# Maxima three steps ahead of the scores, dense couples in the lead-in, pv in pairs at the end

## The chip, the cores and the metric

The kernel runs on one core of one Trainium2 chip. The metric is device time of one execution in microseconds. The kernel before took 1690.04 us as the median of three runs (1687.92 to 1691.31). Names used below: PE is the matrix engine (PEld its weight loads), DVE the vector engine, ACT the scalar engine, POOL the GpSimd engine, SP the engine that issues nearly every DMA, in program order, on one queue.

## What is computed

One transformer block with adaptive layer norm, 2048 tokens of 512 channels, 32 heads of 16 channels, an MLP of 1792:

```python
mod = (_silu(c) @ w_mod).reshape(c.shape[0], 6, 1, -1)
sa, ca, ga, sb, cb, gb = (mod[:, i] for i in range(6))
h = _layernorm(x) * (1 + ca) + sa
q, k, v = split_heads(h @ wqkv)                  # 32 heads of 16
p = _softmax(einsum("bhqd,bhkd->bhqk", q, k) * 16 ** -0.5)
x = x + ga * (merge_heads(einsum("bhqk,bhkd->bhqd", p, v)) @ wo)
h = _layernorm(x) * (1 + cb) + sb
x = x + gb * (mish(h @ w1 + b1) @ w2)            # mish(y) = y * tanh(softplus(y))
```

## The kernel before

**Items and steps.** An item is 512 queries of four heads; there are 32, n = 0 to 31, and each has 16 steps, so t runs from 0 to 511. A step takes 128 keys: four score matmuls of 64 array rows each (L618), one for each head, into four banks of a ring of six PSUM banks; ACT takes the exponential of each bank (L621, tile pr); two steps later the four value matmuls add p·v into the item's accumulator (pv, L636, tiles of 32 columns over all 128 rows).

**Maxima.** The softmax's row maximum is subtracted inside the score matmul: two extra rows of the query tile qa hold its negative as a high and a low part. So an item's maxima must be ready before its first score. They come from a second set of products (max_tile, L569), four to a step, which also go to ring banks and which DVE reduces (L571). Step t makes those of step tm = t + PRO, with PRO = 16 + LEAD, LEAD = 4: maxima run 20 steps ahead. When the last four of an item are reduced, neg_max and max_rows make the rows: a transpose on PE (L598, the only matmul out of ident and mm), ACT writes the high part mh (L600), DVE the low part mt, and four DMAs of SP (L607) put them into qa.

**Dense work beside.** The projections, the output projection and most of the MLP are cut into units of twelve 512-column products. In the main loop a unit is done over two steps as 64-row halves (mm_half, L134; all upper halves in one step, lower ones in the next), a half beside a score or a maximum, as 64-row matmuls in the two halves of the array run together; six slots of a step hold such halves, where there is a unit. Where there is none a step has f = 0: scores stand beside maxima instead, four slots.

**The lead-in.** Steps t = -PRO to -1 have no scores. Each makes two max_pair (L583: two 64-row products into two banks, one DVE reduce L585 over both) and after each step's two pairs whole_units issues CREDIT = 7.2 dense products over all 128 rows (L127). The units there are given by the list plan: slices of v, K and q. When a K or q unit is complete its fin runs: ACT copies the accumulator into qf (L258, one buffer), POOL makes the high part qh and the low part ql (L93, L96, two buffers each), and two hooks later SP writes them out (kscr<-qh and kscr<-ql, L272, L273). Hooks are functions run at a half-step h (two to a step), in order of program; they set the order of the DMAs on SP. Six slices of w1 are split early, in the exponentials' still idle buffers (early_prep, L1488 the load, L1496 the stores).

**What sets the order.** Instructions are written in each engine's order by step(); nothing reorders them. A ring bank is taken in turn, and free_banks, run at the end, removes false dependencies between ring users whose banks differ, looking back over the last 32 of them.

## Time and profile before

| quantity | value |
|---|---|
| median of three runs | 1690.04 us |
| the profiled execution's own time | 1688.32 us |
| its span in the trace | 1686.5 us |
| granted PE clock, mean | 0.999 |
| DMA, mean over the span | 142 GB/s |

The profiled time is the span and 1.8 us around it. Rows of the timeline read: start, duration, engine, line and operation, output <- inputs, array rows*columns for a matmul, shape, count; in brackets the idle time before it and what ended that. A duration of a matmul includes its pipeline, so the cost of one in a stream is read from the distance between starts.

### The profile page before, as it was taken

The page shows a single profiled execution, that of the slowest core. Times are in us where ns is not written, and L with a number is a line of the kernel's source. Part 1 is how long each engine was busy: PE and PEld are TensorE (multiplying, and loading weights), DVE is VectorE, ACT ScalarE, POOL GpSimd, SP SyncE. Part 2 cuts the span into 40 slices and gives each one's busy share as a digit, 9 for nine tenths or more (in the row PEclk, how much of TensorE's full clock was granted, in tenths as well). Part 3 has the DMA queues.
Part 4 walks back from the last instruction along what each step waited for, and adds up shares of the span by engine and source line. Part 5 has one row for each costly group of instructions (what it writes and reads, how often), then busy time and mean ns, then how long its engine had stood idle before and what let it go on. Part 6 is the DMA issues. An engine that isn't in the chain of part 4 may idle for free.

```text
span 1686.5 us, 33920 instructions
## 1 busy us (share of the span) xinstructions
PE 1670.4 (99%) x12491; PEld 924.4 (55%) x12491; DVE 1432.9 (85%) x2372; ACT 1357.4 (80%) x2612; POOL 812.5 (48%) x839
## 2 busy tenths in 40 slices
PE   8999999999999999999999999999999999999998
PEld 6755655555445455555555455555555455555687
DVE  6998888888999988888889888888889888883377
ACT  7257777777778988888878998888878988889674
POOL 5555224655313664556323565556323664555442
PEclk9999999999999999999999999999999999999999
DMA  8877656777755334434355434534344433534261
GB/s 261 264 251 188 157 145 197 205 228 218 225 136 161 97 93 104 120 81 130 82 137 161 106 77 98 139 80 122 100 133 120 130 93 81 149 97 135 76 227 63
DMA packets 114983, 239.00 MB, mean 142 GB/s; under 512 B 24500, under 2 KB 50120, under 8 KB 108864
## 3 DMA queue, kind: packets, MB, share of 16 engines
q1 hardware_dynamic: 114808, 236.82, 49.7%
q8 instruction: 99, 1.62, 0.4%
q14 instruction: 68, 0.56, 0.1%
q10 hardware_dynamic: 8, 0.00, 0.0%
HBM read 180.48 MB, written 51.45 MB: 138 GB/s over the span
## 4 chain that ended last, share of the span: by engine, by line
PE 92%; DVE 3%; ACT 2%; DMA 1%; issue 1%; POOL 0%; SPq 0%; ACTq 0%; DVEq 0%; POOLq 0%
PE bk L636 29%; PE ring L618 22%; PE ring L569 19%; PE bk L134 11%; PE bk L127 3%; PE ring L127 2%; PE ring L1249 2%; DVE mx L571 2%; ACT pr L621 1%; PE ring L583 1%; DMA qa<-mt 0%; PE ring L952 0%; PE ring L598 0%; DMA xt<-in_A_x 0%; PE ring L134 0%
## 5 line engine op out<-in xcount | busy, mean ns | idle before, releaser
L571 DVE TENSOR_REDUCE mx<-ring 128x1 f32<-128x512 f32 x1968 | 1221.9, 681 | 150.9 <-PE ring L569 136.2
L621 ACT ACTIVATE pr<-ring 128x512 f32<-128x512 f32 x2048 | 1078.7, 603 | 207.8 <-PE bk L134 116.3
L569 PE MATMUL ring<-ka,qa 64*128 64x512 f32 x1968 | 818.3, 429 | 1.3 <-ACT pr L621 1.0
L618 PE MATMUL ring<-qa,ka 64*128 64x512 f32 x2048 | 759.0, 402 | 3.2 <-ACT pr L621 2.0
L636 PE MATMUL bk<-pr,vg 128*32 128x512 f32 x4096 | 545.1, 604 | 0.0
L569 PEld LDWEIGHTS ring<-ka,qa 64*128 64x128 f32 x1968 | 350.6, 184 | 326.4 <-DVE mx L571 251.4
L618 PEld LDWEIGHTS ring<-qa,ka 64*128 64x128 f32 x2048 | 373.6, 184 | 192.2 <-DVE mx L571 113.3
L134 PE MATMUL bk<-h,w 64*128 64x512 f32 (+1 forms) x1080 | 277.8, 390 | 0.0
L134 PE MATMUL bk<-w,a_h 64*128 64x512 f32 x632 | 210.8, 413 | 0.0
L134 PEld LDWEIGHTS bk<-h,w 64*128 64x128 f32 x1080 | 178.5, 184 | 9.2 <-ACT pr L621 1.5
L636 PEld LDWEIGHTS bk<-pr,vg 128*32 128x32 f32 x4096 | 81.2, 108 | 135.8 <-issue 126.5
L134 PE MATMUL bk<-w,a_l 64*128 64x512 f32 x316 | 124.0, 392 | 0.0
L134 PEld LDWEIGHTS bk<-w,a_h 64*128 64x128 f32 x632 | 106.7, 184 | 3.4 <-ACT hb L830 0.8
L1008 POOL TENSOR_TENSOR y<-yd,y 128x512 f32<-128x512 f32 x44 | 56.8, 1292 | 88.9 <-ACT yd L1007 79.5
L842 POOL TENSOR_SCALAR qq<-ee 128x512 f32<-128x512 f32 x25 | 15.5, 620 | 169.3 <-ACT ee L836 169.3
L858 POOL TENSOR_TENSOR qq<-qq,rr 128x512 f32<-128x512 f32 x42 | 54.1, 1289 | 85.8 <-ACT rr L852 85.8
L844 POOL TENSOR_TENSOR hb<-hb,ee 128x512 f32<-128x512 f32 x42 | 54.1, 1288 | 79.6 <-DVE ee L840 77.6
L134 PE MATMUL bk<-w,o_hl 64*128 64x512 f32 x288 | 79.3, 405 | 0.0
L96 POOL TENSOR_TENSOR a_l<-hb,a_h 128x512 fp32r<-128x512 f32 x53 | 73.1, 1379 | 4.4
L134 PEld LDWEIGHTS bk<-w,a_l 64*128 64x128 f32 x316 | 58.3, 184 | 2.8
L93 POOL TENSOR_SCALAR qh<-qf 128x512 fp32r<-128x512 f32 x27 | 16.7, 620 | 88.3 <-ACT qf L258 68.1
L134 PE MATMUL bk<-h_h,wl 64*128 64x512 f32 x168 | 57.3, 421 | 0.2 <-ACT pr L621 0.2
(222 smaller groups left out, 1901.3 us busy)
## 6 DMA issues: line engine op xcount, KB each, us to landing
ka<-kscr SPq DMA_DIRECT2D x124, 384.0 KB
w<-w2scr SPq DMA_DIRECT2D x56, 512.0 KB
w<-w1scr SPq DMA_DIRECT2D x46, 512.0 KB
vg<-vscr SPq DMA_DIRECT2D x32, 552.0 KB
qa<-qscr SPq DMA_DIRECT2D x124, 100.0 KB
kscr<-qh SPq DMA_DIRECT2D x16, 512.0 KB
qscr<-qh SPq DMA_DIRECT2D x32, 256.0 KB
w2scr<-hl SPq DMA_DIRECT2D x14, 512.0 KB
```

The source lines that it names most:

```text
L96: (nc.gpsimd if eng == "p" else nc.vector).tensor_sub(lo, src, hi.bitcast(F32))
L127: nc.tensor.matmul(acc, l, r, start=start, stop=stop)
L134: i = nc.tensor.matmul(acc, l[64 * g:64 * g + 64], r[64 * g:64 * g + 64], start=start and not then, stop=bool(stop and then))
L569: nc.tensor.matmul(pm, qt[64 * s:64 * s + 64, qs * P:(qs + 1) * P], kt[64 * s:64 * s + 64, kb * TB:(kb + 1) * TB], start=True, stop=True)
L571: nc.vector.tensor_reduce(out=mxs[n][:, s, 4 * j + qs, kb:kb + 1], in_=pm, op=ALU.max, axis=AX.X)
L618: nc.tensor.matmul(p_, kt[64 * s:64 * s + 64, kc * P:(kc + 1) * P], qt[64 * s:64 * s + 64, :], start=True, stop=True)
L621: e = nc.scalar.activation(pr, p_, AF.Exp, scale=SCALE)
L636: nc.tensor.matmul(accs[n][32 * h:32 * h + 32, :], vgs[n][:, o:o + 32], pts.pop((t, h)), start=(kc == 0), stop=(kc == 15))
L844: (nc.vector if tail else nc.gpsimd).tensor_mul(hb, hb, ee)
L858: nc.gpsimd.tensor_mul(qq, qq, rr)
L1008: nc.gpsimd.tensor_add(y[i], yd, y[i])
L1249: nc.tensor.matmul(po[i // 2][:, i % 2, :], l[:, s], w[:, r, :], start=(f == 0 and j == 0), stop=(f == FT - 1 and j == 2))
```

## The change

- **LEAD is 3.** The maxima lead by 19 steps, the lead-in has 19 steps. As 19 is odd, the couple of steps that share a row block of maxima (tm even, tm odd) no longer coincides with the couple of steps (t even, t odd) that shares a dense unit; the number of maxima that stand alone (others) is kept from the first step of a maxima couple to its second. In item 1 one couple of steps takes its maxima column by column, since half of them were made in the lead-in.
- **Dense work of the lead-in.** whole_units is no longer used there. lanes() yields 64-row half slots, each a pair of matmuls of two accumulators in the two halves of the array; dense_slots takes up to four after every max_pair. Twelve 512-column products make one bank of work (take); two such banks are a couple, which goes through twice: turn(c, 0), and turn(c, 1) with the halves exchanged. Between them a small ACT copy (seen) of a pair of maxima banks is what the second pass waits for. Six couples take the same units as before, four accumulators being in use: two ring banks, "ms" and "acc". The ring has four banks until t = -1.
- **Order of units.** The q unit of plan goes ahead of the twelve v units. Two entries of LATE_SPLIT/LATE_LOAD go away.
- **pv in pairs.** In the last PRO steps (t > T - PRO) a step does no pv at an even t; at an odd t, ahead of the third own score, it does those of t-3 and t-2.
- **Three early slices, not six**, two hooks later; the other three join the chain of start_preps. The windows of clear, store_at and load_at move by two hooks.
- **free_banks looks back over 96** ring users instead of 32.

```diff
-    LEAD = 4
+    LEAD = 3
-    CREDIT = 7.2
-    LATE_SPLIT = {3: -8, 4: 4}
-    LATE_LOAD = {3: -15, 4: -4, 5: 9}
+    LATE_SPLIT = {4: 4}
+    LATE_LOAD = {4: -4, 5: 9}
...
-        b = ring_at[0] % NRING
+        b = ring_at[0] % ring_of[0]
...
-                for j, b, others, theirs in seen[-32:]:
+                for j, b, others, theirs in seen[-96:]:
...
         nc.vector.tensor_reduce(out=mxs[n][:, :, jq, kb:kb + 1], in_=pm, op=ALU.max, axis=AX.X)
+        if waiting:
+            seen = ap.tile([P, 2], F32, tag="seen", name="seen", bufs=2)
+            e = nc.scalar.copy(seen, pm[:, :, 0])
+            for c in waiting:
+                c["after"] = e
+            waiting.clear()
...
+    COUPLES = 6
+    now, waiting = [0], []
+    beds = [ring_t[:, NRING - 2, :], ring_t[:, NRING - 1, :], "ms", "acc"]
+
+    def lanes():
...
+        def turn(c, p):
+            (a, fa), (b, fb) = c["two"]
+            for j, both in enumerate(zip(a, b)):
+                for k in range(max(len(x) for x in both)):
+                    for x, g in zip(both, (p, 1 - p)):
+                        if k < len(x):
+                            mm_half(x[k], g, c["after"] if p and not j and not k else None, p)
+                yield len(a) - j - 1
+            if not p:
+                waiting.append(c)
+                return
+            for fin in fa + fb:
+                at(now[0] + 1, lambda fin=fin, h=now[0] + 1: fin(h))
+
+        for _ in range(COUPLES // 2):
+            c1 = yield from couple()
+            yield from turn(c1, 0)
+            c2 = yield from couple()
+            yield from turn(c2, 0)
+            yield from turn(c1, 1)
+            yield from turn(c2, 1)
...
                 max_pair(tm // 16, jq, kb)
-            if second and tm % 16 == 15:
-                neg_max(tm // 16)
-            run_hooks(2 * t + 1)
+                if i and tm % 16 == 15:
+                    neg_max(tm // 16)
+                if not i:
+                    run_hooks(2 * t + 1)
+                dense_slots(2 * t + 1, 4)
             for f in ats.pop(t, []):
                 f()
-            whole_units(2 * t + 1, CREDIT)
...
         if tm < T:
-            o = max(0, (8 - f) // 2)
+            o = mst["others"] = max(0, (8 - f) // 2) if tm % 2 == 0 or not t else mst["others"]
...
-        mid = False
+        mid = t > T - PRO
...
+            if t > T - PRO and second and i < len(mine) and mine[i] is third:
+                pv(t - 3)
+                pv(t - 2)
...
-    plan = [(-PRO, 2, 0, range(4, 16)), (-PRO, 0, 1, (0,)), (-PRO, 1, 1, range(NB)), (-PRO, 1, 2, range(NB)),
+    plan = [(-PRO, 0, 1, (0,)), (-PRO, 2, 0, range(4, 16)), (-PRO, 1, 1, range(NB)), (-PRO, 1, 2, range(NB)),
...
-    EARLY = 6
+    EARLY = 3
```

New lines shift the numbers: in the kernel after, the scores' exponential is L629 (before L621), the qf copy L260 (L258), mh L608 (L600), the rows of maxima L615 (L607), a maximum's product L571 (L569), a score L626 (L618), pv L644 (L636), a dense half L133 (L134), and the kscr writes L274 and L275 (L272, L273).

Three places show how the order moved. The first is ACT where the main loop begins: after the rows of maxima of item 0 (mh) come the copies of finished units into qf, and the exponentials of the first steps (pr). Before:

```order
L600 ACTIVATE mh<-ring 32x128
L258 COPY qf<-bk 128x512 x3
L621 ACTIVATE pr<-ring 128x512 x8
L89 CAST wh<-wr 128x512
L621 ACTIVATE pr<-ring 128x512 x7
```

And after:

```order
L590 COPY seen<-ring 128x2 x2
L608 ACTIVATE mh<-ring 32x128
L260 COPY qf<-ring 128x512 x2
L260 COPY qf<-bk 128x512 x2
L629 ACTIVATE pr<-ring 128x512 x8
```

Four copies stand ahead of the first exponential instead of three; the last two couples are finished together, so all four belong to units that end at the same place, where before a unit ended every few visits.

The second is SP at the same time. mt are the rows of maxima; vg the first item's values; qa and ka the second pair of queries and keys; wm the first two pieces of w_mod; kscr<-qh and kscr<-ql the writes of finished K units. Before:

```order
L607 DMA qa_101<-mt 2x4x128
L230 DMA wr<-in_A_wqkv 128x4x128
L272 DMA kscr<-qh 128x2x512
L273 DMA kscr<-ql 128x512
L556 DMA vg<-vscr 128x1104
L309 DMA qa_103<-qscr 50x512 x2
L318 DMA ka_701<-kscr 48x2048 x2
L730 DMA wm<-in_w_mod 128x4x256 x2
L272 DMA kscr<-qh 128x2x512
L273 DMA kscr<-ql 128x512
L272 DMA kscr<-qh 128x2x512
```

And after:

```order
L615 DMA qa_101<-mt 2x4x128
L558 DMA vg<-vscr 128x1104
L311 DMA qa_103<-qscr 50x512 x2
L320 DMA ka_701<-kscr 48x2048 x2
L738 DMA wm<-in_w_mod 128x4x256 x2
L274 DMA kscr<-qh 128x2x512
L275 DMA kscr<-ql 128x512
```

The K unit whose write stood between the rows of maxima and the vg load is gone from there: all four remaining K writes (three more such pairs follow these rows) come behind the loads of vg, qa, ka and wm.

The third is PE in the main loop, the first step that has dense halves after steps that had none (t = 128 before, t = 126 after). Before:

```order
L569 MATMUL ring<-ka_701,qa_103 128x512 x2
L134 MATMUL bk<-w_5827,o_hl 128x512
L618 MATMUL ring<-qa_101,ka_99 128x512
L134 MATMUL bk<-w_5827,o_hl 128x512
L569 MATMUL ring<-ka_701,qa_103 128x512
L134 MATMUL bk<-w_5827,o_hl 128x512
L618 MATMUL ring<-qa_102,ka_700 128x512
L134 MATMUL bk<-w_5858,o_hl 128x512
L569 MATMUL ring<-ka_701,qa_103 128x512
L134 MATMUL bk<-w_5858,o_hl 128x512 x2
L618 MATMUL ring<-qa_101,ka_99 128x512
L636 MATMUL bk<-pr,vg 32x512 x4
```

And after:

```order
L133 MATMUL bk<-w_5980,o_hl 128x512
L626 MATMUL ring<-qa_104,ka_702 128x512
L133 MATMUL bk<-w_5980,o_hl 128x512
L626 MATMUL ring<-qa_100,ka_98 128x512
L133 MATMUL bk<-w_5980,o_hl 128x512
L133 MATMUL bk<-w_6009,o_hl 128x512
L626 MATMUL ring<-qa_104,ka_702 128x512
L133 MATMUL bk<-w_6009,o_hl 128x512 x2
L626 MATMUL ring<-qa_100,ka_98 128x512
L571 MATMUL ring<-ka_701,qa_103 128x512 x4
L644 MATMUL bk<-pr,vg 32x512 x4
```

Four maxima that stood between scores and halves now stand by themselves behind the step's halves, just ahead of pv.

More of the change, by code (lines that the diff above doesn't have):

```diff
@@ L147, in adaln_block @@
     ring_at = [0]
+    ring_of = [NRING]
     kept = []
@@ L1308, in whole_units, with take, couple, dense_slots @@
                 cur["fin"] = None
+    COUPLES = 6
+    now, waiting = [0], []
+    beds = [ring_t[:, NRING - 2, :], ring_t[:, NRING - 1, :], "ms", "acc"]
+    def lanes():
+        def take():
+            bed = bank(beds[0])
+            beds.append(beds.pop(0))
+            slots, fins = [], []
+            while len(slots) < 12:
+                while not units or now[0] < units[0][0]():
+                    yield None
+                half = len(fins) * TB // 2
+                unit = units.pop(0)[1]
+                fins.append(unit(bed[:, half:]))
+                n = 2 if pe_queue[0][0].shape[-1] <= TB // 2 else 1
+                ms = [(*m[:3], m[3] and half == 0, m[4] and len(slots) * n + len(pe_queue) == 12 * n) for m in pe_queue]
+                slots += [ms[j:j + n] for j in range(0, len(ms), n)]
+                pe_queue.clear()
+            return slots, fins
+        def couple():
+            a = yield from take()
+            b = yield from take()
+            return {"two": (a, b)}
+        def turn(c, p):
[18 more added lines that the diff above has]
+            yield from turn(c2, 1)
+    lane = lanes()
+    def dense_slots(h, most):
+        now[0] = h
+        for _ in range(most):
+            if not next(lane, 0):
+                return
     def maxima(n, u, s, others):
         j, qs = divmod(u, 4)
+        if (n, u) == (1, PRO % 16 // 2):
+            return ([max_tile(n, j, v, qs, kb) for kb in (2, 3)] for v in (s, 1 - s))
         return ([max_tile(n, j, s, qs, kb) for kb in range(4 - others)],
```

25 lines of the change are left out of this document (18 added, 7 removed).

## The prediction

> **What bounds the kernel now.** I read the page first, for the engine that never rests and for the chain that ended last.
>
> ```profile
> span 1686.5 us, 33920 instructions
> ...
> PE 1670.4 (99%) x12491; PEld 924.4 (55%) x12491; DVE 1432.9 (85%) x2372; ACT 1357.4 (80%) x2612; POOL 812.5 (48%) x839
> ...
> PE bk L636 29%; PE ring L618 22%; PE ring L569 19%; PE bk L134 11%; PE bk L127 3%; PE ring L127 2%; PE ring L1249 2%; DVE mx L571 2%; ACT pr L621 1%; PE ring L583 1%; DMA qa<-mt 0%; PE ring L952 0%; PE ring L598 0%; DMA xt<-in_A_x 0%; PE ring L134 0%
> ```
>
> PE is the bound, and the chain is made of PE instructions. So an edit costs what it adds to PE's slots or what it makes PE wait for. Then I took the stretches that the change touches, as windows: the lead-in; the vg issue to the first wm in use; five congested microseconds; the last steps. Columns are microseconds, busy time of PE, PEld, DVE, ACT and POOL, the granted clock, the DMA share and GB/s.
>
> ```profile
> 47.46:98.95 51.49, 51.37 (x298) 36.61 (x298) 47.55 (x44) 9.82 (x22) 29.87 (x28) 1.00 0.84 274
> 96.16:108.72 12.56, 11.94 (x77) 7.06 (x75) 11.57 (x17) 8.14 (x16) 5.09 (x6) 1.00 1.02 280
> 460.00:465.00 5.00, 4.79 (x31) 1.95 (x30) 4.72 (x10) 4.15 (x9) 0.00 (x0) 1.00 1.01 367
> 1532.00:1584.20 52.20, 52.20 (x397) 25.82 (x400) 8.03 (x13) 45.81 (x89) 30.37 (x29) 1.00 0.21 72
> ```
>
> The lead-in takes 51.49 us with PE full and DVE nearly; in the second stretch the DMA engines are full (share 1.02); in the last, PE is full again.
>
> **1. The lead-in gets shorter, by about 5.5 us.** The unit of cost is the distance between starts in PE's timeline, and DVE's reduce.
>
> ```profile
> 89.26 0.28 PE L598 MATMUL ring<-ident,mm 128*32 128x128 f32 x1
> ...
> 98.95 0.50 PE L618 MATMUL ring<-qa,ka 64*128 64x512 f32 x1
> ...
> 111.69 1.06 PE L636 MATMUL bk<-pr,vg 128*32 128x512 f32 x8
> 112.69 0.50 PE L569 MATMUL ring<-ka,qa 64*128 64x512 f32 x1
> ...
> 113.03 0.39 PE L618 MATMUL ring<-qa,ka 64*128 64x512 f32 x1
> ...
> 113.26 0.39 PE L569 MATMUL ring<-ka,qa 64*128 64x512 f32 x1
> ...
> 114.58 1.07 PE L636 MATMUL bk<-pr,vg 128*32 128x512 f32 x8
> ```
>
> ```profile
> L585 DVE TENSOR_REDUCE mx<-ring 128x2 f32<-128x1024 f32 x40 | 46.9, 1219 | 3.1 <-PE ring L583 2.5
> ```
>
> A slot of two 64-row matmuls costs 113.26 - 113.03 = 0.23 us. After, a visit is one max_pair (one slot) and four dense slots: 5 x 0.23 to 0.24 = 1.18 us on PE; DVE needs 46.9 / 40 = 1.17 us for its reduce, so the two run level. Before, a visit takes 51.49 / 40 = 1.29 us: the dense work is the same, but changes of shape between 64 and 128 rows go away. There are 38 visits instead of 40. The dense work, 144 slots, lasts for 36 of them: 36 x 1.18 = 42.5; of the last two, bare pairs that DVE limits (2 x 1.17), PE runs one ahead: 1.2. One new stall stands against it. The weights of the first large K unit (wl) are split on POOL behind the early slices:
>
> ```profile
> 63.54 0.62 POOL L93 TENSOR_SCALAR ep<-ep 128x512 fp32r<-128x512 f32 x1 [8.22 <-DMA ep<-in_B_w]
> ...
> 74.43 1.29 POOL L96 TENSOR_TENSOR wl<-wr,wh 128x512 fp32r<-128x512 f32 x1 [3.01 <-ACT wh L89]
> ```
>
> The q unit comes first and the v units follow, so the K unit is wanted at visit 16, 47.5 + 16 x 1.18 = 66.4. POOL gets the first early slice at 63.5, then has a high part (0.62) and a low part (1.29, as wl's) for it, as much for the q unit, and wl: 63.5 + 1.95 + 1.95 + 1.3 = 68.7, gaps included. Stall 2.2 us. So PE begins step 0 at 47.46 + 42.5 + 1.2 + 2.2 = 93.4 instead of 98.95: -5.5 us. Without the stall it would be -7.7, with DVE setting every visit and none run ahead -4. Item 0's transpose stands behind visit 34: 47.46 + 34 x 1.18 + 2.2 = 89.8 (before 89.26).
>
> **2. Then the main loop waits, which eats that and costs 11 us more.** ACT has four qf copies ahead of the first exponential. qf has one buffer, so the last copy waits for POOL's low part of the unit before it; that low part stands on POOL behind the same unit's high part; qh has two buffers, so that high part waits for a DMA, the kscr write of the unit two back. On SP this write now stands behind vg, qa, ka and wm. PE can issue its first dozen products of step 0, then the ring is full of scores that nothing has read. SP, POOL and ACT at this place before:
>
> ```profile
> 91.77 2.79 SPq L607 DMA_DIRECT2D qa<-mt  x4
> ...
> 95.16 0.45 SPq L272 DMA_DIRECT2D kscr<-qh  x1
> ...
> 96.16 1.01 SPq L556 DMA_DIRECT2D vg<-vscr  x1
> ...
> 99.17 1.62 SPq L730 DMA_DIRECT2D wm<-in_w_mod  x2
> 100.88 0.78 SPq L272 DMA_DIRECT2D kscr<-qh  x1
> ```
>
> ```profile
> 100.04 0.62 POOL L93 TENSOR_SCALAR qh<-qf 128x512 fp32r<-128x512 f32 x1 [1.89 <-DMA kscr<-qh]
> ...
> 108.72 1.89 POOL L734 TENSOR_TENSOR wm<-wm,sil 128x1024 f32<-128x1024 f32 x1 [2.32 <-DMA wm<-in_w_mod]
> ```
>
> ```profile
> 99.13 0.59 ACT L258 COPY qf<-bk 128x512 f32<-128x512 f32 x1 [3.06 <-PE bk L127]
> 99.62 2.07 ACT L621 ACTIVATE pr<-ring 128x512 f32<-128x512 f32 x4
> ```
>
> ```profile
> ka<-kscr SPq DMA_DIRECT2D x124, 384.0 KB
> ...
> vg<-vscr SPq DMA_DIRECT2D x32, 552.0 KB
> qa<-qscr SPq DMA_DIRECT2D x124, 100.0 KB
> kscr<-qh SPq DMA_DIRECT2D x16, 512.0 KB
> ...
> wm<-in_w_mod SPq DMA_DIRECT2D x8, 512.0 KB
> ```
>
> The POOL row at 100.04 shows the dependency at work before: a high part that waits 1.89 us for the kscr write of 95.16, the one that stood ahead of vg. The exponentials did not care, since the last copy (99.13) was already done. After, the transpose at 89.8 lets SP issue the rows of maxima 2.5 us later (as 91.77 against 89.26), 2.8 us long, and vg at 95.2. From the vg issue to the first wm in use was 108.72 - 96.16 = 12.56 us before, with a write of 768 KB (95.16 and its low part) still ahead in the queue, which at the 280 GB/s of that window is 2.8 us: 9.8 us without it. Behind the first wm come the second and the write, 512 KB each: 1.05 MB / 280 = 3.7 us. So the write has landed at 95.2 + 9.8 + 3.7 = 108.7. POOL's high and low part take 1.95, ACT's copy 0.6: first exponential at about 111.2, against 99.62. That is +11.6; since PE has most of step 0 done by then, about 0.6 comes back: **+11.0 us** for the main loop against before, the gain of part 1 included. By the 367 GB/s of the best window the same sum gives 9.6 - 2.1 + 2.9 = 10.4 from the vg issue, first exponential at 108.1, +8. With the queue slower than 280 by a tenth and the transpose 1.5 us later it is +14. I keep +6 to +14, and take 280 as it is this very stretch.
>
> By the Trainium skill ("DMA: Bandwidth & Descriptors", section "Anatomy of one DMA"), whose fit is for DMAs issued by GpSimd, one DMA takes about 2.0 us and its bytes at 436 GB/s. As an estimate by that page the 3.1 MB from vg to the write would land 9.2 us after the vg issue, the first exponential would come at 107.0, and the sum of part 2 would be +7 instead of +11. No window here moved 436 GB/s; the fullest shows 367.
>
> **3. Ten-slot steps: +3.9 us.** Where dense work comes back after steps without it, five times in the loop, the kept number of lone maxima leaves a step with six dense slots and four maxima behind them: 10 slots instead of 7. 5 x 3 x 0.23 = 3.45. At the five opposite changes a step without dense has 7 slots instead of 4:
>
> ```profile
> L571 DVE TENSOR_REDUCE mx<-ring 128x1 f32<-128x512 f32 x1968 | 1221.9, 681 | 150.9 <-PE ring L569 136.2
> ```
>
> ```profile
> 439.29 1.06 PE L636 MATMUL bk<-pr,vg 128*32 128x512 f32 x8
> ...
> 442.01 1.07 PE L636 MATMUL bk<-pr,vg 128*32 128x512 f32 x8
> ```
>
> Such a step takes 2.72 us, nearly a full one's 114.58 - 111.69 = 2.89, though it has four slots fewer; DVE's four reduces (681 ns each in the group's row, 2.72 us) set it. Seven slots, the values (1.0) and some 0.2 for changes of shape (part 4) are 2.81: +0.09 each, +0.45. If waiting DVE and ACT already leave room in a ten-slot step, +1; if the four lone maxima queue at DVE, each 0.68, less 4 x 0.23 of PE, +7.
>
> **4. The end: -1.5.** The lead-in has one step of maxima less, so the loop has one step more that carries them, 2.89 us instead of the 2.59 that these rows show: +0.3. And pv in pairs takes one stretch of values in two away, on some 9 pairs of steps.
>
> ```profile
> 1543.06 1.07 PE L636 MATMUL bk<-pr,vg 128*32 128x512 f32 x8
> ...
> 1545.65 1.06 PE L636 MATMUL bk<-pr,vg 128*32 128x512 f32 x8
> ```
>
> Going over to values and back costs what the starts beside it lie further apart than 0.23: 113.03 - 112.69 = 0.34 behind the values, some 0.1 more than a slot, and I take as much ahead of them: 0.2. 9 x 0.2 = -1.8. PE is busy 52.20 of 52.20 us there, ACT 45.81, so PE's gain counts, unless eight values at once leave the ring full: -2.5 to -0.5.
>
> **5. Item boundaries: +1.** Between the rows of maxima and the item's first score there are now two steps, not three.
>
> ```profile
> 1022.68 0.28 PE L598 MATMUL ring<-ident,mm 128*32 128x128 f32 x1
> ...
> 1031.49 0.49 PE L618 MATMUL ring<-qa,ka 64*128 64x512 f32 x1
> ```
>
> ```profile
> 1023.66 2.76 SPq L607 DMA_DIRECT2D qa<-mt  x4
> ```
>
> From transpose to score it was 8.8 us; now 5.9. The fourth DMA is issued 3.7 us after the transpose, which leaves 2.2 for it to land. That holds on an empty queue. Where the queue is full it was late already:
>
> ```profile
> 369.97 7.91 DMA qa<-mt
> ```
>
> That row of the chain (start, duration) is an item whose rows came after 7.91 us. The step less makes such an item up to 2.9 later; two or three lie in the congested stretch, some of it hidden: +1, from 0 to +5. Three early slices fewer move 2.3 MB of loads and stores out of the lead-in into the chain of preparations, which ends long before its results are needed: 0. The longer look-back can only remove waits; I count 0 here and give it a rival.
>
> Sum against the profiled execution: 11.0 + 3.9 + 0.3 - 1.8 + 1 = +14.4, or 1688.3 + 14.4 = 1702.7. The median of the runs lies 1.7 above the profiled one: 1704. What the measurement can tell from no change is about 0.2%, 3.4 us.
>
> **Rivals.**
> - B, no stall: the exponentials are not held, as the write lands before it is wanted. The main loop then starts 5.5 us early, -5.5 + 3.9 + 0.3 - 1.8 + 1 = -2.1: 1688. Against it stands the order on SP and the full queue; for it only that PE could run late enough, which would need vg's issue 10 us ahead of the last copy.
> - C, faster: the look-back of 96 frees false waits. A step with dense takes 2.89 us; its seven slots, the values (112.69 - 111.69 = 1.0) and 0.2 for the changes of shape make 7 x 0.23 + 1.2 = 2.81. Over some 470 such steps that is -38 at most; with the stall, half of it (-19) decides and gives 1685, and on top of B a tenth gives 1684. Against it: PE stands idle for 16 us of the whole span (1686.5 - 1670.4), and the waits freed must be on users more than 32 back.
> - D, much slower: the rows of maxima come late at every item. From 5.9 us on for the landing, each boundary waits; with 1 us at 20 items +20, 1724; at most 2.9 x 31 = +90. For it: 7.91 us in one item. Against it: 3.7 us of issue leave 2.2 to land on most.
>
> **How the numbers follow.** A (stall of 6 to 14 us, 1697 to 1710) 0.70, since its chain of waits is written in the order and its price is from the same stretch; B 0.10; C 0.08; D 0.12. Range: 1690 to 1714, which leaves out C, half of B and half of D beyond it. Faster by over 0.2%: C and half of B, 0.12; within: half of B and a mild stall, 0.06; slower: the rest, 0.82.
>
> **What would show it.** After, PE's timeline has a gap of over 10 us in step 0, ended by ACT pr, and ACT's qf copy ahead of it is released by POOL ql, and POOL's qh by DMA kscr<-qh. Step 0's first score is near 93.4. Five steps have four maxima alone and take 3.6 us. The chain holds DMA qa<-mt at a few items only. If the gap is missing, B holds; if steps in the middle are shorter than 2.89, C; if each item's first score waits, D.

## The result

The kernel after takes 1739.97 us (median; 1734.42 to 1743.09), the kernel before 1690.0: a ratio of 1.0297, 95% interval 1.0275 to 1.0319. It is 50 us slower, where 14 were forecast and 1714 was the end of the range. The page of the profile after:

```profile
span 1738.2 us, 34382 instructions
...
PE 1682.5 (97%) x12707; PEld 942.1 (54%) x12707; DVE 1434.4 (83%) x2373; ACT 1360.7 (78%) x2619; POOL 812.2 (47%) x839
...
PE 86%; DVE 5%; DMA 3%; ACT 3%; SPq 1%; issue 1%; POOL 0%; ACTq 0%; DVEq 0%; POOLq 0%
PE bk L644 28%; PE ring L626 20%; PE ring L571 19%; PE bk L133 12%; DVE mx L573 2%; ACT pr L629 2%; PE ring L1257 2%; PE ring L126 1%; PE bk L126 1%; DVE mx L587 1%; DMA kscr<-qh 1%; DMA qa<-mt 1%; DMA wr<-in_A_wqkv 0%; DMA kscr<-ql 0%; PE ring L960 0%
```

The same chain by engine before:

```profile
PE 92%; DVE 3%; ACT 2%; DMA 1%; issue 1%; POOL 0%; SPq 0%; ACTq 0%; DVEq 0%; POOLq 0%
```

PE's busy time grew by 12 us, its idle time from 16 to 56, and DMA, ACT and DVE hold more of the chain. Cut at the starts of the values (pv) of a few steps, the two profiled executions differ like this (us):

| stretch | before | after | more |
|---|---|---|---|
| start to the first values | 106.0 | 125.4 | +19.4 |
| values 0 to 112 | 325.7 | 334.6 | +8.9 |
| values 112 to 480 | 1072.5 | 1080.2 | +7.7 |
| values 480 to 511 | 80.0 | 95.7 | +15.7 |
| the rest | 102.3 | 102.2 | -0.1 |

**The start.** PE's timeline of the kernel after, with the waits in brackets:

```profile
66.92 0.38 PE L133 MATMUL bk<-wh,h_h 64*128 64x256 f32 x1 [0.51 <-ACT vq L289]
...
71.74 0.79 PE L133 MATMUL bk<-h_h,wl 64*128 64x512 f32 x1 [2.83 <-POOL wl L95]
...
88.69 2.07 PE L133 MATMUL bk<-h_h,wh 64*128 64x512 f32 x7 [1.59 <-ACT wh L88]
...
97.01 0.28 PE L606 MATMUL ring<-ident,mm 128*32 128x128 f32 x1
...
105.00 0.39 PE L571 MATMUL ring<-ka,qa 64*128 64x512 f32 x1
118.43 1.22 PE L571 MATMUL ring<-ka,qa 64*128 64x512 f32 x2 [13.03 <-ACT pr L629]
```

ACT, POOL and SP at the same place:

```profile
88.02 0.62 ACT L88 CAST wh<-wr 128x512 fp32r<-128x512 f32 x1 [4.32 <-DMA wr<-in_A_wqkv]
...
117.29 0.59 ACT L260 COPY qf<-bk 128x512 f32<-128x512 f32 x1 [13.84 <-POOL ql L95]
117.77 2.07 ACT L629 ACTIVATE pr<-ring 128x512 f32<-128x512 f32 x4
```

```profile
115.29 0.62 POOL L92 TENSOR_SCALAR qh<-qf 128x512 fp32r<-128x512 f32 x1 [12.46 <-DMA kscr<-qh]
```

```profile
80.58 0.43 SPq L232 DMA_DIRECT2D wr<-in_A_wqkv  x1
...
104.08 0.84 SPq L274 DMA_DIRECT2D kscr<-qh  x1
```

The chain that was forecast is there link by link: the write of 104.08, POOL's high part, ACT's copy, the first exponential, and PE idle for 13.03 us. But the transpose came at 97.0 instead of 89.8.

**The end.** PE, then ACT, in two steps with a pair of values:

```profile
1576.72 1.92 PE L644 MATMUL bk<-pr,vg 128*32 128x512 f32 x16
1578.57 0.50 PE L626 MATMUL ring<-qa,ka 64*128 64x512 f32 x1
...
1582.81 0.49 PE L133 MATMUL bk<-w,a_h 64*128 64x512 f32 x1 [0.61 <-ACT pr L629]
...
1583.69 1.92 PE L644 MATMUL bk<-pr,vg 128*32 128x512 f32 x16
```

```profile
1576.29 1.07 ACT L629 ACTIVATE pr<-ring 128x512 f32<-128x512 f32 x2
1579.11 1.08 ACT L629 ACTIVATE pr<-ring 128x512 f32<-128x512 f32 x2 [1.75 <-PE ring L626]
```

Two steps take 1583.69 - 1576.72 = 6.97 us; before they took 5.24. ACT has two exponentials left when PE turns to the values, and then stands for 1.75 us. Later PE stands for ACT.

**The five changes between steps with and without dense work.** PE at the first return of dense work:

```profile
493.40 1.08 PE L571 MATMUL ring<-ka,qa 64*128 64x512 f32 x4
494.42 1.06 PE L644 MATMUL bk<-pr,vg 128*32 128x512 f32 x8
```

The four lone maxima stand where the order put them. From the values before to these it is 4.16 us, against 3.33 at the same place before. PE and then ACT where dense work had just ended, the opposite change:

```profile
464.79 1.07 PE L644 MATMUL bk<-pr,vg 128*32 128x512 f32 x8
...
468.37 1.07 PE L644 MATMUL bk<-pr,vg 128*32 128x512 f32 x8
```

```profile
466.31 3.05 ACT L629 ACTIVATE pr<-ring 128x512 f32<-128x512 f32 x6 [1.06 <-PE ring L626]
```

This step has seven slots and takes 3.58 us, in which ACT works through six exponentials without a break; a step of four slots took 2.72 before (442.01 - 439.29 in the prediction's rows). DVE and PE in that step of before, each with a wait:

```profile
440.85 2.48 DVE L571 TENSOR_REDUCE mx<-ring 128x1 f32<-128x512 f32 x4 [0.25 <-PE ring L569]
```

```profile
441.46 0.50 PE L618 MATMUL ring<-qa,ka 64*128 64x512 f32 x1 [0.22 <-ACT pr L621]
```

**The rows of maxima.** Two rows of the chain, items 5 and 6:

```profile
347.05 4.65 DMA qa<-mt
...
398.64 5.16 DMA qa<-mt
```

### The profile page after: what moved, and what is told of

Same layout as the page of the kernel before. It is cut to its first block, busy times and chain, and to the rows that moved or that the text cites. A ratio compares the mean times of both kernels' runs of the same rounds, so it can differ in the third digit from the quotient of the medians.

```text
span 1738.2 us, 34382 instructions
## 1 busy us (share of the span) xinstructions
PE 1682.5 (97%) x12707; PEld 942.1 (54%) x12707; DVE 1434.4 (83%) x2373; ACT 1360.7 (78%) x2619; POOL 812.2 (47%) x839
## 4 chain that ended last, share of the span: by engine, by line
PE 86%; DVE 5%; DMA 3%; ACT 3%; SPq 1%; issue 1%; POOL 0%; ACTq 0%; DVEq 0%; POOLq 0%
PE bk L644 28%; PE ring L626 20%; PE ring L571 19%; PE bk L133 12%; DVE mx L573 2%; ACT pr L629 2%; PE ring L1257 2%; PE ring L126 1%; PE bk L126 1%; DVE mx L587 1%; DMA kscr<-qh 1%; DMA qa<-mt 1%; DMA wr<-in_A_wqkv 0%; DMA kscr<-ql 0%; PE ring L960 0%
## 5 line engine op out<-in xcount | busy, mean ns | idle before, releaser
L629 ACT ACTIVATE pr<-ring 128x512 f32<-128x512 f32 x2048 | 1082.2, 603 | 243.9 <-PE bk L133 128.4
L571 PE MATMUL ring<-ka,qa 64*128 64x512 f32 x1972 | 817.6, 429 | 14.7 <-ACT pr L629 14.2
L626 PE MATMUL ring<-qa,ka 64*128 64x512 f32 x2048 | 763.2, 404 | 10.8 <-DMA qa<-mt 7.7
L571 PEld LDWEIGHTS ring<-ka,qa 64*128 64x128 f32 x1972 | 352.0, 184 | 359.7 <-DVE mx L573 265.2
L644 PE MATMUL bk<-pr,vg 128*32 128x512 f32 x4096 | 544.3, 605 | 0.0
L626 PEld LDWEIGHTS ring<-qa,ka 64*128 64x128 f32 x2048 | 376.1, 185 | 174.2 <-DVE mx L573 89.6
L133 PE MATMUL bk<-h,w 64*128 64x512 f32 (+1 forms) x1080 | 278.2, 390 | 2.2 <-ACT pr L629 1.5
L133 PE MATMUL bk<-w,a_h 64*128 64x512 f32 x632 | 211.5, 414 | 7.3 <-ACT pr L629 5.9
L133 PEld LDWEIGHTS bk<-h,w 64*128 64x128 f32 x1080 | 178.3, 184 | 12.3 <-ACT pr L629 5.4
L644 PEld LDWEIGHTS bk<-pr,vg 128*32 128x32 f32 x4096 | 82.1, 108 | 137.7 <-issue 128.6
L133 PE MATMUL bk<-w,a_l 64*128 64x512 f32 x316 | 124.3, 393 | 0.0
L133 PEld LDWEIGHTS bk<-w,a_h 64*128 64x128 f32 x632 | 106.3, 184 | 15.7 <-ACT pr L629 10.8
L133 PE MATMUL bk<-w,o_hl 64*128 64x512 f32 x288 | 78.8, 405 | 0.0
L133 PE MATMUL bk<-h_h,wl 64*128 64x512 f32 x192 | 64.2, 432 | 3.1 <-POOL wl L95 2.8
L133 PEld LDWEIGHTS bk<-w,a_l 64*128 64x128 f32 x316 | 58.3, 184 | 3.8
L133 PE MATMUL bk<-h_h,wh 64*128 64x512 f32 x192 | 55.5, 424 | 3.4 <-ACT wh L88 1.6
```

Source lines behind the costliest of these rows:

```text
L133: i = nc.tensor.matmul(acc, l[64 * g:64 * g + 64], r[64 * g:64 * g + 64], start=start and not then, stop=bool(stop and then))
L571: nc.tensor.matmul(pm, qt[64 * s:64 * s + 64, qs * P:(qs + 1) * P], kt[64 * s:64 * s + 64, kb * TB:(kb + 1) * TB], start=True, stop=True)
L626: nc.tensor.matmul(p_, kt[64 * s:64 * s + 64, kc * P:(kc + 1) * P], qt[64 * s:64 * s + 64, :], start=True, stop=True)
L629: e = nc.scalar.activation(pr, p_, AF.Exp, scale=SCALE)
L644: nc.tensor.matmul(accs[n][32 * h:32 * h + 32, :], vgs[n][:, o:o + 32], pts.pop((t, h)), start=(kc == 0), stop=(kc == 15))
```

## The experiments

Every run is compared with runs of the kernel before on the same chip (1688 to 1690 us). Beside the median stands where the profiled time went, by the stretches of the table above, in us more than before; the last column is the MLP behind the values. The profiled execution can lie up to 5 us from the median (a_late 1736.6, a_evenpv 1736.0, a_evenw 1722.2).

| run | median | start | 0-112 | 112-480 | 480-511 | rest |
|---|---|---|---|---|---|---|
| after | 1740.0 | +19.4 | +8.9 | +7.7 | +15.7 | -0.1 |
| a_single | 1723.2 | +17.7 | +9.1 | +7.5 | +1.3 | 0.0 |
| b_pairs | 1705.3 | -0.4 | -1.0 | +0.4 | +16.5 | 0.0 |
| a_evenpv | 1731.8 | +17.3 | +13.7 | +7.7 | +8.9 | +0.1 |
| a_late | 1732.5 | +11.9 | +12.9 | +7.6 | +15.7 | +0.1 |
| a_wr | 1735.2 | +12.8 | +8.0 | +7.7 | +15.8 | -0.1 |
| a_roomy | 1722.7 | -0.3 | +11.6 | +7.8 | +15.7 | -0.1 |
| a_even | 1737.7 | +11.4 | -0.3 | +2.6 | +21.0 | +15.4 |
| a_evenw | 1726.8 | +9.6 | +7.9 | +0.2 | +16.5 | -0.2 |
| a_even6 | 1721.0 | +17.8 | -1.2 | +0.1 | +16.5 | -0.1 |
| a_early6 | 1738.8 | +17.4 | +8.8 | +7.7 | +15.7 | -0.4 |
| b_look96 | 1688.8 | -0.3 | +0.1 | +0.2 | +0.1 | 0.0 |
| best4 | 1687.6 | -3.4 | +3.7 | +0.2 | 0.0 | -0.1 |
| best6 | 1687.5 | +0.5 | -1.2 | -0.1 | 0.0 | 0.0 |
| best3 | 1707.7 | +1.3 | +7.7 | +7.9 | +1.3 | 0.0 |
| lead3_win | 1701.6 | +1.2 | +0.4 | +7.6 | +1.3 | +0.2 |

The first two columns scatter. Item 0's transpose, up to which after, a_single, a_evenpv, a_late and a_roomy are the same, comes at 97.0, 94.0, 94.5, 97.1 and 93.5 us; the first values of the first three differ by 2.1 us; and the column 0-112 is +8.9, +9.1 and +13.7 in them, though their order does not differ there either. So single differences under 4 us in the column of the start, and under 5 us in the column 0-112, mean nothing by themselves. The other columns repeat to some tenths.

### The pairs of values

**a_single**, the kernel after with one step's values a visit:

```diff
-        mid = t > T - PRO
+        mid = False
...
-            if t > T - PRO and second and i < len(mine) and mine[i] is third:
-                pv(t - 3)
-                pv(t - 2)
```

> The kernel after, with the values of the last steps one step at a time again, at the end of each step; nothing else changed. Theory (place of the pair): in the kernel after two steps at the end take 6.98 us where they took 5.25 us before, because the pair of values stands right behind PE's wait for ACT and before the third score, so ACT runs out of scores while PE does 1.85 us of values. Then the last 18 steps come back to 2.6 us each: 9 x 1.73 = -15.6 us against the kernel after, about 1724 us. Rival (the step less of maxima or the dense halves of the last steps make it, not the pairs): no change, 1740 us.

**b_pairs**, the kernel before with the pairs alone:

```diff
+            third = own[2]
...
-        mid = False
+        mid = t >= T - PRO
...
+            if t >= T - PRO and second and i < len(mine) and mine[i] is third:
+                pv(t - 3)
+                pv(t - 2)
```

> The kernel before, with only the pairs of values in its last 20 steps. Theory (place of the pair): +1.73 us for each of 10 pairs, about 1690 + 17 = 1707 us. Rival (as the prediction had it, pairs save changes of shape, and something else lengthens the end of the kernel after): 1688 to 1690 us.

Measured: 1723.2 us (-16.8 against after) and 1705.3 us (ratio to before 1.0099, interval 1.0082 to 1.0115). Both by the theory. The pairs cost 14 us in after (the last steps fall from +15.7 to +1.3) and 16.5 in the kernel before, which has ten of them and not nine: about 1.6 us a pair, wherever the rest of the change is or is not. A window of 56 us in the last steps, of after and then of a_single (span, PE, PEld, DVE, ACT, POOL, clock, DMA share, GB/s), shows the two engines give way together:

```profile
1576.00:1632.00 56.00, 47.05 (x324) 23.18 (x325) 5.66 (x9) 39.14 (x74) 23.43 (x22) 1.00 0.20 67
```

```profile
1560.00:1616.00 56.00, 55.92 (x423) 28.34 (x419) 13.87 (x24) 49.33 (x96) 31.91 (x31) 1.00 0.24 83
```

PE is busy 47.05 us with pairs and 55.92 without, ACT 39.14 and 49.33: neither is full with pairs, since they wait for each other in turn.

**a_evenpv**, the pairs moved to the end of the even steps:

```diff
-            if t > T - PRO and second and i < len(mine) and mine[i] is third:
-                pv(t - 3)
-                pv(t - 2)
...
         if not mid:
             pv(t - 2)
+        elif t > T - PRO and not second:
+            pv(t - 2)
+            pv(t - 1)
```

> The kernel after with the pairs of values kept, but moved to the end of the even steps (those of t-2 and t-1 behind the fourth score), ahead of the odd step's wait for ACT. Theory (it is the place, not the pairing): four scores are then queued for ACT, 4 x 0.52 = 2.1 us of work against 1.85 us of values, so ACT does not run dry; two steps at the end take 5.0 to 5.3 us and the time falls by 15 to 17 us, 1723 to 1725 us. Rival (eight values in a row starve ACT wherever they stand): 1735 to 1740 us.

Measured 1731.8 us, between the two. The last steps lose 8.9 us instead of 15.7, or 7.6 of 14.4 without the 1.3 that a_single keeps. PE, then ACT:

```profile
1590.71 1.92 PE L644 MATMUL bk<-pr,vg 128*32 128x512 f32 x16
...
1595.21 0.50 PE L133 MATMUL bk<-h,w 64*128 64x512 f32 x1 [0.77 <-ACT pr L629]
```

```profile
1593.09 3.26 ACT L629 ACTIVATE pr<-ring 128x512 f32<-128x512 f32 x6 [1.16 <-PE ring L626]
```

So the place makes about half of it, and the row of eight values the other half: ACT still stands for 1.16 us, and the dense halves, which must wait for an exponential between their two passes, wait for ACT later. The theory of the place alone falls.

### The wait for the K write

**a_late**, the loads behind the rows of maxima moved back, so that the write stands directly behind vg:

```diff
-                at(max(0, h + 2), lambda: first_mods(max(0, h + 2)))
+                at(max(4, h + 2), lambda: first_mods(max(4, h + 2)))
...
-    for pp, h in ((2, -22), (3, -2)):
+    for pp, h in ((2, -22), (3, 3)):
```

> The kernel after, with the loads of the second pair of item 1 (qa, ka) moved five hooks later and the first pieces of w_mod four hooks later, so that the four last K writes stand directly behind the vg load on SP. Theory (the write holds the exponentials): the write is issued at about 101.5 us instead of 104.1 and lands with 1 MB ahead of it instead of 3 MB, near 106.5 us; first exponential at about 108.6 instead of 117.8: -9 us, 1731 us. Rival 1 (the exponentials wait for the chain of copies through POOL itself): at most -3 us, 1737 us. Rival 2 (the loads moved back hold item 1's maxima instead): the gap moves to about 115 to 125 us and the gain is under 4 us.

**a_roomy**, buffers of their own for the last K units, with the order as it is:

```diff
+            spare = {(1, 1, 3): 0, (1, 2, 0): 1}.get((kind, ct, tb))
...
+            else:
+                if not spare:
+                    spares.append(ap.tile([P, DK, TB], F32R, tag="o_0", name="o_hl", bufs=1))
+                qh, ql = spares[0][:, 2 * spare, :], spares[0][:, 2 * spare + 1, :]
...
+                idle = {(1, 1, 2): 0, (1, 1, 3): 2}.get((kind, ct, tb))
...
+                else:
+                    qf = ap.tile([P, TB], F32, tag=f"p{idle}", name="qf", bufs=3)
```

> The kernel after with buffers of their own for the last two K units of the lead-in (high and low parts in the output projection's still idle tile, two of the qf copies in idle exponential buffers); order of all instructions and DMAs unchanged. Theory (the exponentials wait for the K write through qh, ql and qf): no copy waits for a write any more; the first exponential starts about 1 us after the first scores, near 105 us instead of 117.8: -12 us, 1728 us. Rival (the vg load behind the same DMA queue, or the rows of maxima, hold the first steps anyway): the gap moves to the first values at step 2, gain under 5 us.

Measured 1732.5 us (-7.5) and 1722.7 us (-17.3); as ratios to before 1.0262 and 1.0216, against 1.0297 for after. The chain of a_late, and ACT's timeline of a_roomy:

```profile
101.46 5.23 DMA kscr<-qh
...
109.32 2.08 ACT pr L629 x4
```

```profile
98.05 1.07 ACT L272 COPY qf<-bk 128x512 f32<-128x512 f32 x2 [3.03 <-PE bk L133]
99.26 2.06 ACT L641 ACTIVATE pr<-ring 128x512 f32<-128x512 f32 x4
```

With the write behind vg alone the first exponential comes at 109.3, 8.5 us earlier than in after (forecast 108.6). With buffers of their own the copies wait for nothing but PE, the exponentials begin at 99.3, and the first values come 19.7 us earlier, more than was expected; 3.5 us of this are the transpose, which came earlier in that execution. From the transpose to the first exponential it is 20.8 us in after, 12.3 in a_late and 5.8 in a_roomy: that is free of the scatter, and the wait is shown. It goes through the buffers and the write, not through the copies themselves. In both runs 0-112 is 3 to 4 us longer than in after; since a_evenpv has as much with nothing changed there, whether some of the gain is given back is not shown.

**a_wr**, the load of the second K slice ahead of the second pair's loads:

```diff
-    LATE_LOAD = {4: -4, 5: 9}
+    LATE_LOAD = {3: -24, 4: -4, 5: 9}
```

> The kernel after with one entry put back: the load of the second K slice (wr) stands on SP ahead of the second pair's qa and ka loads instead of behind them. Theory: in the kernel after this load landed at 88.0 us, PE waited 1.6 us for the weights and then ran at a granted clock of 0.6 for 4 us; with the load early both go, item 0's transpose comes 3 us earlier, and so do the wait for the K write and the main loop: -3 us, 1737 us. Rival (the lead-in is held by DVE or the wait for the write swallows it): 0, 1740 us.

Measured 1735.2 us, 4.8 less than after (expected -3), but as a ratio to before 1.0285 (1.0263 to 1.0307) against 1.0297 (1.0275 to 1.0319): the intervals overlap, and the times do not show a gain. The trace shows the step. In after this load was issued at 80.58 and the cast that needed it started at 88.02; in a_wr the cast starts at 80.29, PE does not wait for it, and the transpose comes at 90.5, ahead of the 93.5 to 97.1 of the kernels that are the same up to there. So a part of the late transpose was this load, 3 us at least in this execution.

### The lead of 19 steps

**a_even**, LEAD = 4 and what goes with it (the windows of before, no column order in item 1, and ten pairs of values at the end):

```diff
-    LEAD = 3
+    LEAD = 4
...
-        return h if h < 60 or h % 32 < 27 else h - h % 32 + 34
+        return h if h < 60 or h % 32 < 25 else h - h % 32 + 34
...
-        if (n, u) == (1, PRO % 16 // 2):
-            return ([max_tile(n, j, v, qs, kb) for kb in (2, 3)] for v in (s, 1 - s))
```

> The kernel after with LEAD = 4 again: 20 steps of lead, so the couples of maxima and of steps coincide, no ten-slot steps, three steps between the rows of maxima and the first score; the windows of the stores and loads as before. Theory: the seven microseconds at the five returns of dense work go away (7.4 us more than before in t = 114 to 434), and so do the late rows at items 5 and 6 (9.5 us); one step of maxima more in the lead-in is hidden by the wait for the K write; the last steps keep their pairs. About -16 us, 1724 us. Rival (items 5 and 6 are late because of the three early slices that moved into the congested stretch, not because of the step less): only -7 us, 1733 us.

Measured 1737.7 us, hardly less than after, and not by either theory. The table tells why: t = 0 to 112 did lose its 9 us, but the 15.4 us came up in the MLP. By the trace, with three early slices and the windows of before dense work comes back at step 138 instead of 126; 30 steps are without dense halves instead of 22, and 8 x 6 = 48 half slots are left for the end. The run does not tell the parts apart. So two more were made in which the steps without dense work stay 22:

**a_evenw**: as a_even, but with the windows of after. **a_even6**: as a_even, with six early slices at their old hooks. **a_early6**: the kernel after, LEAD = 3, with those six slices.

```diff
-    EARLY = 3
+    EARLY = 6
...
-        at(3 * i - 35, lambda i=i: early_prep(i, 3 * i - 35))
+        at(3 * i - 37, lambda i=i: early_prep(i, 3 * i - 37))
```

> The kernel after with LEAD = 4, this time with the store and load windows of the kernel after, so that the MLP opens at the same step (t = 120) and the same steps have no dense halves. Theory: t = 112 to 160 and 272, 400 lose the 7 us of the ten-slot steps, items 5 and 6 the 7 to 9 us of late rows; in the lead-in one step more is hidden by the wait for the K write: -16 us, 1724 us. Rival (late items 5 and 6 come from three early slices fewer): -7 us, 1733 us.

> The kernel after with LEAD = 4, the store and load windows of before, and six early slices again: of the change only the dense couples of the lead-in (with the order of units), the look-back and the pairs of values are left. Theory: the stretch between the lead-in and the last steps is as long as before (within 1 us); the first values come 11 to 12 us late, since the exponentials still wait for the K write; the pairs cost 17 us: 1690 + 28 = 1718 us. Rival (the couples or the look-back cost something in the middle): over 1722 us.

> The kernel after with six early slices instead of three, LEAD = 3 and its windows kept. Theory (items 5 and 6 begin late because the three slices moved behind them delay SP and the DMA queues there): the 9 us that t = 0 to 96 take more than before fall to about 2: -7 us, 1733 us. Rival (the step less between the rows of maxima and the first score makes them late): t = 0 to 96 stays at +7 to +9 us, 1738 to 1741 us.

Measured: 1726.8, 1721.0 and 1738.8 us. In a_even6 the first values come 17.8 us late, where 11 to 12 were expected; PE waits 3.42 us for a K slice there. All three agree on 112-480: +7.7 with LEAD = 3 and +0.1 or +0.2 with LEAD = 4, so the lead of 19 steps costs 7.5 us there. In the kernel after 6.2 us of it lie in the steps of the five changes, where the couples no longer coincide, and 1.0 in one step at the start of item 27. On the late rows they were a surprise: three or six slices make no difference (8.8 and 8.9), but LEAD = 4 alone does not cure it either (a_evenw, 7.9); only with the windows of before does it go (a_even6, -1.2; a_even, -0.3). So neither theory held, and the windows, which I had taken for a detail, were the next suspect. The early slices are not free in every kernel, though: a_even and a_even6 differ in them alone, by 17 us. With the windows of before, dense work comes back at step 138 with three slices and at 128 with six; with the windows of after, at 126 with three (a_evenw).

**best3** and **lead3_win**: LEAD = 3 in a kernel without the other costs (single values, early wr, own buffers, six early slices behind the first large K slice, the modulation two steps later), and the same with the windows of before, the three functions two hooks earlier again.

> The same kernel with LEAD = 3 and its windows, column order in item 1 and kept lone maxima: against the other of this call it shows what the lead of 19 steps costs by itself. Theory: the lead-in ends 2.4 us earlier, the ten-slot steps cost 7, the late rows at items 5 to 7 cost 8 to 10: +12 to +15 us against the other, 1697 to 1700 us. Rival (the late rows were a result of the late start, whose transfers piled up behind it): +5 us, 1690 us.

> The last kernel with a lead of 19 steps, with one thing put back: the windows in which stores and loads of the weights' preparation may be issued are those of before, two hooks earlier in the item. In the last kernel the load of a raw slice (hl) stood on SP ahead of vg, qscr and the rows of maxima of items 5 to 7, and waited there for its buffer; with the windows of before it stands behind them. Theory (the moved windows make the rows late): t = 0 to 112 falls from +7.7 us against before to +1 to +4, what the step less leaves; about 1703 us. Rival (the step less alone makes them late): +7 to +8 as it was, 1707 us.

Measured 1707.7 and 1701.6 us; best3 is 8 us above what was expected, lead3_win near it. About half of the 8 is a lead-in that did not get shorter, since PE waits in both for a K slice that POOL splits (best3):

```profile
87.34 2.07 PE L133 MATMUL bk<-h_h,wl 64*128 64x512 f32 x7 [4.22 <-POOL wl L95]
```

In 0-112 the windows take +7.7 to +0.4, as they did with LEAD = 4 (a_evenw +7.9, a_even -0.3). The chain of best3 and then of lead3_win, a long row each of the rows of maxima:

```profile
330.70 4.47 DMA qa<-mt
```

```profile
373.92 5.57 DMA qa<-mt
```

SP of the kernel after ahead of item 6, and SP's waits in the window 380 to 400 us, show what holds them:

```profile
387.96 0.59 SPq L682 DMA_DIRECT2D rb<-rscr  x1
391.52 0.33 SPq L776 DMA_DIRECT2D hl<-in_B_w  x1
...
394.37 2.00 SPq L783 DMA_DIRECT2D w2scr<-hl  x1
396.47 5.53 SPq L615 DMA_DIRECT2D qa<-mt  x4
```

```profile
SPq L776 <- DMA w2scr<-hl: 6.1, 2, 3.5
```

A load of the weights' preparation (hl) stands ahead of vg, qscr and the rows, and holds SP from 388.5 to 391.5 until an earlier store out of hl has landed, which frees its buffer. DVE had the rows ready at 393.2; SP reaches them 3.25 us later, and the four small DMAs then take 5.53 us to issue instead of 2.8. PE waits 5.67 us for them. In best3 it is the same at item 5, with smaller sizes: the load holds SP from 321.7 to 323.3, the rows start 1.6 us after DVE has made them and take 5.02 us to issue. In lead3_win a store and the load still stand ahead of the rows at item 5, unlike what I had expected, but the load stands behind vg and qscr and no longer waits for its buffer, both are issued before the rows are due, and the rows take 2.77:

```profile
322.10 1.49 SPq L795 DMA_DIRECT2D woscr<-hl  x1
323.69 1.74 SPq L788 DMA_DIRECT2D hl<-in_B_w  x1
326.98 2.77 SPq L627 DMA_DIRECT2D qa<-mt  x4
```

The step less between rows and score, with the windows of before, leaves +0.4 us in 0-112: alone it was not the cause. Against the same kernel with LEAD = 4 (best6, below) LEAD = 3 costs 20 us with its windows and 14 without them. The wait of 4.2 to 4.4 us for the K slice is in both figures.

### The look-back

**b_look96**: the kernel before with `seen[-96:]`.

> The kernel before with a look-back over 96 ring users instead of 32, nothing else. Theory (the waits it frees were never last): no change, 1688 to 1690 us. Rival (it frees false waits in the steps with dense halves): steps of 2.84 instead of 2.84 and 2.90 in turn, up to -10 us, 1680 us.

Measured 1688.8 us, ratio 1.0001 (0.9991 to 1.0010): nothing.

### The couples alone

**best4** is the kernel after with LEAD = 4 and the windows of before, single values, the early wr load, the buffers of a_roomy, and six early slices at `3 * i - 31`. **best6** has beside it the first matmuls of the modulation two steps later.

> The dense couples of the lead-in without what came with them: LEAD = 4, windows of before, values one step at a time, six early slices but four hooks later (behind the first large K slice's split on POOL), the second K slice loaded early, and the buffers of their own for the last two K units. Theory: 40 visits at 1.18 us from 48.3 us, no wait for weights or for the K write: step 0 at 95.5 to 96.5 us instead of 98.95; everything behind as before: -2 to -3.5 us against before, 1685 to 1687 us. Rival (another wait takes the place, the vg load or the rows of maxima): 1689 us or more.

> The previous kernel of the couples alone, with the first matmuls of the modulation two steps later. In the previous one the first values came 3.4 us ahead of before, and 4.2 us were given back in one step, in which PE waited for POOL's sums over the first pieces of w_mod. Theory: without that wait the 3.4 us stay, 1684.5 to 1685.5 us. Rival (the shorter lead-in always runs into a transfer, and another wait gives it back): 1687 us or more.

Measured 1687.6 us (0.9992, 0.9982 to 1.0002) and 1687.5 us (0.9995, 0.9986 to 1.0004): no difference that can be measured. In best4 the first values came 3.4 us early, and a wait took it back. PE there:

```profile
120.30 0.30 PE L126 MATMUL ring<-wm,ones 128*32 128x128 f32 x2 [2.79 <-POOL wm L756]
```

In best6 that wait is gone (0-112: -1.2), but in its profiled execution the lead-in began later (48.85), and step 0 with it (98.51). That is 49.7 us from the first pair to step 0, against 51.5 before; in best4 it was 48.1. So the couples do shorten the lead-in by 2 to 3 us in these profiles, but no run of a whole kernel was faster beyond its interval.

## Why the prediction was wrong

The forecast had the sign; the profiled execution took 51.6 us more than before where the sum had 14.4. Of the 37 us between them the end makes 17.2, the start 8.4, the item boundaries 7.9 and the changes of dense work 3.8. Of five terms one was right in its mechanism and close in its size, one was half right, and three missed most.

- **Part 1 (lead-in, "PE begins step 0 at 93.4").** The price of a visit was right: the 15 visits from 48.29 to 65.95 take 1.18 us each. The wait for wl was there, 2.83 us (2.2 forecast). The step that failed is "one new stall stands against it": there was another for the K slice loaded by wr (1.59 us) and a small one for ACT's copies of v (0.51 and 0.17), and after each of the two long waits PE ran at a lower clock for 3 to 4 us. Together with a start 0.8 us later the transpose came at 97.0, not 89.8; in other executions of the same order it came from 93.5 on. a_wr shows the part of the load.
- **Part 2 (wait, +11; the start measured +19.4).** From the transpose to the first exponential 111.2 - 89.8 = 21.4 us were forecast and 117.77 - 97.01 = 20.8 measured. a_roomy and a_late show the cause. That the sizes agree so well is in part luck: vg was issued 4.0 us behind the transpose, not 5.4, and from there to POOL's release it took 14.3 us, not 13.5. The sum was short because the transpose that it starts from was 7 us late, and because the way from the first exponential to the first values, where 0.6 us were to come back, took 1.2 us more than before.
- **Part 3 (+3.9; measured +7.7).** The places were right, the sizes were not. The five ten-slot steps took 0.83, 0.41, 0.25, 0.48 and 0.47 us more than the same places before, 2.4 in sum, where 3.45 were taken. The step that failed is the price of the five steps of seven slots, "+0.09 each, +0.45": they took 0.85, 0.85, 1.07, 0.51 and 0.50 more, 3.8 in sum. The reading behind it, that DVE's four reduces set the 2.72 us of a step without dense work, does not hold: in the two rows of before above they take 2.48 us, DVE stands for PE and PE for an exponential. So PE's three slots more were not covered by DVE; 3 x 0.23 = 0.69 us would be their own price, and what makes the rest of each step is not shown.
- **Part 4 (-1.5; measured +15.7).** The wrong sign, and the largest miss. The step that failed is "PE is busy 52.20 of 52.20 us there, ACT 45.81, so PE's gain counts". ACT at 88% has little room; what counts is how many scores it has left when PE leaves for 1.85 us. The pair was put behind a wait of PE for ACT, where two are left. The order shows that place; I priced the changes of shape and did not follow ACT's queue. The other term there, +0.3 for one step more with maxima, was small too: a_single, best3 and lead3_win keep +1.3 without the pairs.
- **Part 5 (+1; measured +8.9).** I priced the step less and left the windows of the stores and loads out of the sum. lead3_win and a_even show the windows to be nearly all of it. Rival D had the effect, but at every item and from the wrong cause.
- The early slices and the look-back were costed at nothing. a_early6 shows that for the slices in the kernel after, b_look96 for the look-back in the kernel before; with the windows of before three slices instead of six do cost (a_even against a_even6).
- A slip in the chances: C and half of B are 0.08 + 0.05 = 0.13, not 0.12.

## What to carry to other kernels

When work is moved on a full engine, follow the queue of the engine that it feeds: an average load of 88% does not tell whether it runs dry in the 1.85 us for which nobody feeds it. When a table of times is shifted beside a larger change, price it as a change of its own: on a queue that issues in order, a load that waits for its buffer holds everything behind it, a small urgent transfer too. And a wait whose cause is a buffer is best tested by giving the buffer, as that leaves the order alone.

## What the hardware showed that was not expected

PE's granted clock can fall after a wait of a few microseconds. In windows of the kernel after, behind the waits of 2.83, 1.59 and 13.03 us:

```profile
71.70:74.70 3.00, 2.96 (x20) 2.97 (x22) 0.43 (x1) 0.00 (x0) 2.83 (x4) 0.50 0.68 210
...
88.60:92.60 4.00, 3.91 (x22) 3.12 (x24) 1.24 (x2) 0.20 (x2) 1.28 (x1) 0.59 0.99 336
...
117.70:121.70 4.00, 3.02 (x10) 2.00 (x12) 1.83 (x3) 2.83 (x7) 1.89 (x2) 0.50 0.87 326
...
350.00:354.00 4.00, 2.17 (x18) 1.46 (x22) 1.63 (x3) 1.88 (x5) 3.27 (x4) 1.00 0.69 240
```

The clock, the number ahead of the DMA share, is 0.50 or 0.59 in the first three for 3 to 4 us; as an estimate from 3 us at half clock, the wait of 2.83 us thus cost about 1.5 us more. It does not fall every time: the last window holds the wait of 2.04 us for the rows of item 5, and the clock stays 1.00. What tells these waits apart is not shown. The kernel before has a mean clock of 0.999 over its span, the kernel after 0.992. The Trainium skill ("TensorE: Matmul & The Clock Gate", section "Part 1: The HAM clock gate (the "warmup" mystery)") says that PE runs at half clock after about one idle window of 3.4 us and at full clock again after as long a busy one. The half clock and its length agree with these rows; the waits behind which it came were shorter here, 2.83 and 1.59 us, the first within 5.7 us of which PE was busy for 2.23.
